# The last output of a state-space scan with a maxout layer: the products of the differences first, and four separate places for the result

## The chip, the cores and the metric

The kernel runs on one core of a Trainium2 chip. Its time is the device time of one execution in microseconds (us). The core has five engines with a queue of instructions each: TensorE (PE in the profile; its weight loads are listed apart, as PEld), VectorE (DVE), ScalarE (ACT), GpSimd (POOL) and SyncE (SP, which here issues the transfers). Matmuls write to PSUM, an accumulator memory of eight banks of 128 partitions by 2 KB; the other data are in SBUF. Transfers to and from the main memory go over 16 DMA engines. The profile is of one execution, and its times are counted from the start of the span, that is from the first recorded instruction.

## The reference

Two layers follow each other. The first is a scan over 768 tokens of 4 sequences with 8 heads, done in chunks; the second is a feed-forward layer that takes the maximum of three projections:

```python
# first layer, for each chunk, in outline
y[:, :, sl] = y_intra + y_inter              # (batch 4, heads 8, seq 768, head_dim 32)
state = decay_full * state + sum_j(B_j x_j decay_from_j)

# bridge: 4 x 768 tokens of 8 * 32 = 256 numbers
x = y.transpose(0, 2, 1, 3).reshape(3072, 256)

# second layer: w1, w2, w3 are 256 x 768, w_out is 768 x 256
h = np.maximum(np.maximum(x @ w1, x @ w2), x @ w3)
out = h @ w_out                              # 3072 x 256, float32
```

The change touches only the last product, `h @ w_out`, and only for the last 128 tokens of each of the four sequences.

## The kernel before

The kernel takes the 768 tokens in six chunks of 128 (`NC = 6`, `c = 0` to 5). A chunk holds 128 tokens of all four sequences (`NB = 4`), 512 in all. For each chunk it scans, makes the three projections in 36 units, takes the maximum (tiles `m`, 128 by 512, with four buffers), and makes six tiles of hidden values (`NF = 6`, 128 hidden values by 512 tokens each). Then come the products with `w_out`. The order of the work on every engine is the order of the program; it is written out by hand in short words (`FIRST`, `SECOND`, `STEADY`, `LAST`), and semaphores hold an instruction back until its data and its place are there.

From chunk 1 on, products are made from split operands. A hidden tile (`hidden`, L642) becomes three: a high part `hi` = value times a number just below one (ScalarE, L645), a low part `lo` = value less `hi` (VectorE, L648), and a difference `d` = `hi` less `lo` divided by TAU (VectorE, L639). The weights have the same three parts. In the code they are numbered 0 (`hi`), 1 (`lo`) and 2 (`d`). The result is (products of parts 0 and 1, less KAPPA times the products of part 2), times BACK; KAPPA and BACK are constants.

For chunks 1 to 4, "Y" steps make the products of part 2, ScalarE scales the bank in place, and "X" steps add the products of parts 0 and 1; `put` scales and stores. The last chunk's output is made by `last_down` (L787). It has one PSUM bank for each sequence, as two halves of 128 tokens by 256 outputs: `o[:, 0]` collects the products of parts 0 and 1, `o[:, 1]` those of part 2. It goes twice over the four sequences: first with hidden tiles 0 to 3 (12 matmuls for each sequence), then with tiles 4 and 5 (6 for each). In the second round each sequence is finished in turn:

- ScalarE reads `o[:, 0]`, scales it and writes it to `ob` in SBUF (L802),
- VectorE reads `o[:, 1]`, scales it, adds `ob`, and writes `ob` (L803),
- SP issues a store of 128 by 256 numbers, 128 KB (L806).

The tag "ob" has two buffers, so sequences 0 and 1 write to two places, and sequences 2 and 3 to the same two again. The tag "m" has four buffers, one taken by each hidden tile in turn; the last four takers before `last_down` are hidden tiles 2, 3, 4 and 5. Nothing follows `last_down` in the program.

Of the kernel before, what the change touches and what calls it, by code (L numbers as in the profile page):

```python
# [9 lines left out]
FP32 = mybir.dt.float32  # L10
# [3 lines left out]
AF = mybir.ActivationFunctionType  # L14
ALU = mybir.AluOpType
# [5 lines left out]
def kernel(  # L21
# [20 lines left out]
    nc = tc.nc  # L42

    NB, NH, S, D = x.shape
    N = B.shape[-1]
    P = 128
# [7 lines left out]
    DM, DF = moe_w1.shape  # L54
    KD = DM // P
    NF = DF // P
    BLK = NB * P
# [14 lines left out]
    KAPPA = TAU / (1.0 + TAU)  # L72
    HIGH = 1.0 - 2.0 ** -13
    BACK = ((1.0 + TAU) / TAU) ** 2
# [9 lines left out]
    ffn = ctx.enter_context(tc.tile_pool(name="ffn", bufs=2))  # L84
# [17 lines left out]
    def att_bank(shape, name):  # L102
        turn["att"] += 1
        if shared["att"] and turn["att"] % 5 == 0:
            return bank("sumA", 1, shape, name)
        return bank("att", 4, shape, name)

    def ffn_bank(shape, name):
        turn["ffn"] += 1
        if shared["ffn"] and turn["ffn"] % 3:  # L110
            return bank("sumB", 2, shape, name)
        return bank("ffn", 1, shape, name)
# [4 lines left out]
    for k in range(REP):  # L117
# [5 lines left out]
        out=a_sb,  # L123
        in_=a_rows.rearrange("r (c i) -> (r c) i", i=P).rearrange("(w r) i -> r w i", w=2))
# [4 lines left out]
            name=nc.get_next_instruction_name(),  # L129
# [23 lines left out]
    NW = 3 * NQ  # L153
# [22 lines left out]
    hs, h0 = {}, {}  # L176
# [103 lines left out]
    def weight_part(k, j, row, cols):  # L280
        return parts[k][j][:, row, cols]
# [14 lines left out]
        out=pick, in_=ident.rearrange("p (r k) -> p k r", k=BH), op=ALU.add, axis=AX.X)  # L296
    npick = const.tile([P, BH], FP32, name="npick")
    nc.vector.tensor_scalar(
        out=npick, in0=pick, scalar1=-1.0, scalar2=None, op0=ALU.mult)
# [4 lines left out]
        out=hsel, in_=hsel, pattern=[[-N, NH]], compare_op=ALU.is_ge, fill=0.0,  # L304
        base=0, channel_multiplier=1)
    nc.gpsimd.affine_select(
        out=hsel, in_=hsel, pattern=[[N, NH]], compare_op=ALU.is_ge, fill=0.0,
# [3 lines left out]
        out=parity, in_=hsel.rearrange("p (r g) -> p g r", g=2), op=ALU.add, axis=AX.X)  # L311
# [6 lines left out]
        out=mask, in_=mask, pattern=[[1, P]], compare_op=ALU.is_ge, fill=MASKED,  # L318
# [377 lines left out]
    opened, m, ready = {}, {}, set()  # L696
# [51 lines left out]
    def tokens(b):  # L748
        return slice(b * P, (b + 1) * P)
# [37 lines left out]
    def last_down():  # L787

        c = NC - 1
        os_ = [att_bank([P, 2, DM], "o") for _ in range(NB)]  # L790
        for fs in (range(NF - 2), range(NF - 2, NF)):
            for b, o in enumerate(os_):
                for f in fs:
                    for p in (2, 0, 1):
                        nc.tensor.matmul(  # L795
                            out=o[:, p // 2], lhsT=hs[f][p][:, tokens(b)],
                            rhs=weight_part(NW + f // 2, p, f % 2, slice(0, DM)),
                            start=(f == 0 and p == 2), stop=(f == NF - 1 and p > 0),
                            skip_group_check=True)
                if fs[-1] == NF - 1:  # L800
                    ob = ffn.tile([P, 2, DM], FP32, tag="ob", name="ob")[:, 0]
                    nc.scalar.activation(ob, o[:, 0], AF.Copy, scale=BACK)  # L802
                    nc.vector.scalar_tensor_tensor(  # L803
                        out=ob, in0=o[:, 1], scalar=-KAPPA * BACK, in1=ob, op0=ALU.mult,
                        op1=ALU.add)
                    nc.sync.dma_start(  # L806
                        out=out.rearrange("(b s) m -> s b m", s=S)[c * P:(c + 1) * P, b], in_=ob)

    for b in range(2, NB):
        below(b)  # L810
# [20 lines left out]
        out=cums.rearrange("k c s -> (k c) s").rearrange("(w r) s -> r w s", w=2), in_=a_sb)  # L831
# [219 lines left out]
    for n in range(NF * 3):  # L1051
        j, g = divmod(n, 2)
        q, i = divmod(j, 3)
        f = 2 * q + g
# [7 lines left out]
        if j > 0:  # L1062
            p = ffn_bank([P, BLK], "up")
            whole_group(p, i, f)
        else:
            p = pair[g]
# [3 lines left out]
        else:  # L1070
            if i == 2:
                h0[f] = hidden_place(NF - 2 + f // 3, f % 3, FP32)
            nc.vector.tensor_tensor(
                out=m[g] if i == 1 else h0[f], in0=m[g], in1=p, op=ALU.max)
# [22 lines left out]
    for steps in (tops, tails):  # L1097
        while steps:
            take(steps)
    last_down()  # L1100


# [28 lines left out]
```

## Time and profile before

| what | us |
|---|---|
| median of 4 runs (lowest, highest) | 279.46 (278.15, 282.49) |
| the profiled execution's own time | 279.69 |
| its span, first to last instruction | 277.9 |
| TensorE busy | 262.6 (94%) |
| ScalarE busy | 187.8 (68%) |
| VectorE busy | 180.7 (65%) |
| GpSimd busy | 72.1 (26%) |
| ScalarE's step of the last output, each of four (L802) | 0.383 |
| VectorE's step of the last output, each of four (L803) | 0.424 |
| last four stores, from issue to landing | 1.7 |

The busy times overlap, since the engines work side by side; a share of the span says little by itself. What sets the end is the chain of waits: it is followed back from the last instruction, at each step to what released it. A row of the chain or of the timeline gives the start in us from the start of the span, the length in us, the engine, the line of the kernel and the tile. "PE o L795" is a matmul into the banks of the last output, "ACT ob L802" and "DVE ob L803" are the two steps after it. In a view of waits, a row gives who waited, on whom, the sum in us, how often, and the longest. In a table of windows, a row has the stretch, its length, the busy time and the number of instructions of PE, PEld, DVE, ACT and POOL, the granted clock of TensorE, the mean share of the DMA engines that was busy, and the GB/s that they moved.

### The profile page before, as it was taken

The numbers are of one execution on the slowest core, as the hardware profiler recorded it, in microseconds if no ns is written. First come the engines' busy times: TensorE is split into PE (matmuls) and PEld (weight loads), VectorE is DVE, ScalarE is ACT, GpSimd is POOL, SyncE is SP. The second block draws the span as 40 slices with busy tenths as digits, with TensorE's granted clock in tenths as the row PEclk, the third lists the DMA queues.
The fourth block names the chain that finished last, engine by engine and source line by source line (L and its number), as shares of the span: only waits on it lengthen the run. The fifth ranks groups of instructions, "written<-read, shape, count | busy, mean of one in ns | idle before, by whom it ended". The sixth has DMA issues, their size and how long they took to land.

```text
span 277.9 us, 5404 instructions
## 1 busy us (share of the span) xinstructions
PE 262.6 (94%) x2054; PEld 205.4 (74%) x2054; DVE 180.7 (65%) x292; ACT 187.8 (68%) x423; POOL 72.1 (26%) x72
## 2 busy tenths in 40 slices
PE   6886799999999999999999999999999999999992
PEld 4663344438887787889888889888789788898892
DVE  2584577999476699573478852578760876713942
ACT  2774759891999999936699745799653854425612
POOL 5173915555973362216000333000000000000000
PEclk9999599999999999999999999999999999999999
DMA  7989989979992285688340793200001100002002
GB/s 83 179 290 287 283 138 167 224 171 224 173 230 55 62 97 72 91 203 125 95 62 0 146 239 32 78 0 2 1 0 40 39 2 0 0 2 75 2 0 75
DMA packets 105049, 28.13 MB, mean 101 GB/s; under 512 B 75328, under 2 KB 101952, under 8 KB 105024
## 3 DMA queue, kind: packets, MB, share of 16 engines
q1 hardware_dynamic: 104720, 27.66, 48.9%
q8 instruction: 16, 0.26, 0.4%
q10 hardware_dynamic: 304, 0.13, 0.2%
q14 instruction: 9, 0.07, 0.1%
HBM read 24.54 MB, written 3.24 MB: 100 GB/s over the span
## 4 chain that ended last, share of the span: by engine, by line
PE 85%; DMA 6%; ACT 3%; DVE 3%; issue 1%; ACTq 0%; SPq 0%; DVEq 0%
PE up L728 30%; PE up L706 15%; PE o L770 12%; PE up L665 7%; PE o L765 4%; PE y L598 3%; DMA rb<-in_moe_w_dram 3%; PE s L566 3%; PE o L795 3%; PE y L589 2%; DMA cums<-a_sb 2%; PE spread L396 1%; PE trB L493 1%; PE trC L493 1%; PE A L534 1%
## 5 line engine op out<-in xcount | busy, mean ns | idle before, releaser
L728 PE MATMUL up<-six,wp 128*128 128x512 f32 x360 | 95.8, 393 | 0.0
L728 PEld LDWEIGHTS up<-six,wp 128*128 128x128 f32 x360 | 66.6, 188 | 14.7 <-ACT six L625 0.6
L742 DVE TENSOR_TENSOR m<-m,up 128x512 f32<-128x512 f32 x60 | 40.4, 684 | 46.7 <-PE up L728 46.1
L692 ACT ACTIVATE up<-up 128x512 f32<-128x512 f32 x90 | 50.9, 582 | 19.5 <-PE up L706 19.3
L706 PE MATMUL up<-six,wd 128*128 128x512 f32 x180 | 53.9, 399 | 0.0
L467 ACT ACTIVATE L<-L,ncums 128x128 f32<-128x128 f32 x160 | 50.3, 394 | 0.0
L706 PEld LDWEIGHTS up<-six,wd 128*128 128x128 f32 x180 | 32.7, 188 | 8.7 <-DVE m L742 1.9
L574 DVE TENSOR_TENSOR L<-s,L 128x512 f32<-128x512 f32 x46 | 30.0, 682 | 2.1 <-issue 1.3
L665 PE MATMUL up<-six,w 128*128 128x512 f32 x64 | 30.8, 632 | 0.0
L460 POOL TENSOR_SCALAR_AFFINE_SELECT L<-L 128x1024 f32<-128x1024 f32 x20 | 21.9, 1120 | 12.4 <-DMA L<-cums 12.4
L770 PE MATMUL o<-wp,h 128*128 128x256 f32 x192 | 23.7, 283 | 0.0
L770 PEld LDWEIGHTS o<-wp,h 128*128 128x128 f32 x192 | 23.4, 192 | 0.1
L665 PEld LDWEIGHTS up<-six,w 128*128 128x128 f32 x64 | 12.7, 205 | 14.5 <-issue 13.5
L225 POOL TENSOR_TENSOR h<-h,h 128x512 uint32<-128x512 uint32 x12 | 16.1, 1345 | 23.8 <-DVE h L219 18.5
L639 DVE SCALAR_TENSOR_TENSOR h<-h,h 128x512 fp32r<-128x512 f32 x30 | 20.8, 692 | 1.0
L648 DVE TENSOR_TENSOR h<-m,h 128x512 fp32r<-128x512 f32 x30 | 20.8, 694 | 0.0
L645 ACT ACTIVATE h<-m 128x512 fp32r<-128x512 f32 x30 | 18.5, 629 | 3.0 <-DVE m L742 3.0
L783 ACT ACTIVATE ob<-o 128x512 f32<-128x512 f32 x10 | 6.0, 597 | 19.9 <-PE o L770 16.2
L566 PE MATMUL s<-six,six 32*128 32x256 f32 x192 | 15.2, 401 | 1.4 <-ACT six L508 1.4
L740 DVE COPY m<-up 128x512 f32<-128x512 f32 x14 | 9.6, 689 | 9.2 <-PE up L728 9.1
L566 PEld LDWEIGHTS s<-six,six 32*128 32x128 f32 x192 | 9.8, 184 | 6.7 <-issue 3.6
L770 PEld LDWEIGHTS o<-wd,h 128*128 128x128 f32 x96 | 12.6, 190 | 0.6
(101 smaller groups left out, 319.7 us busy)
## 6 DMA issues: line engine op xcount, KB each, us to landing
L<-cums SPq DMA_DIRECT2D x10, 1024.0 KB, 10.5
rb<-in_moe_w_dram SPq DMA_DIRECT2D x9, 512.0 KB, 6.4
raw_x<-in_x_dram SPq DMA_DIRECT2D x6, 512.0 KB, 10.4
out_dram<-ob SPq DMA_DIRECT2D x10, 256.0 KB, 2.1
raw_B<-in_B_dram SPq DMA_DIRECT2D x6, 256.0 KB, 4.5
raw_C<-in_C_dram SPq DMA_DIRECT2D x6, 256.0 KB, 6.3
rb<-in_moe_w_out_dram SPq DMA_DIRECT2D x3, 512.0 KB, 4.8
E<-cums SPq DMA_DIRECT2D x40, 32.0 KB, 2.4
```

What stands on the lines that cost most here:

```text
L460: nc.gpsimd.affine_select(out=Ls[c][:, b], in_=Ls[c][:, b], pattern=[[0, NH], [1, P]], compare_op=ALU.is_ge, fill=MASKED, base=0, channel_ ...
L467: nc.scalar.activation(L[:, b, h], L[:, b, h], AF.Exp, bias=ncum[c][:, b * NH + h:b * NH + h + 1], scale=1.0)
L566: nc.tensor.matmul(out=s[:, i].rearrange("j g i -> j (g i)"), lhsT=st["BT"][rows, b], rhs=st["CT"][rows, :, b], start=(i == 0), stop=True, ...
L574: nc.vector.tensor_tensor(out=M, in0=s, in1=M, op=ALU.mult)
L639: nc.vector.scalar_tensor_tensor(out=out, in0=lo.bitcast(FP32), scalar=-1.0 / TAU, in1=hi.bitcast(FP32), op0=ALU.mult, op1=ALU.add)
L648: nc.vector.tensor_tensor(out=lo, in0=src, in1=hi.bitcast(FP32), op=ALU.subtract)
L665: nc.tensor.matmul(out=bank, lhsT=whole[3 * (f // 2) + i][:, k, f % 2 * P:(f % 2 + 1) * P], rhs=yT[0][:, k], start=(k == 0), stop=(k == KD ...
L692: nc.scalar.activation(bank, bank, AF.Copy, scale=-KAPPA)
L706: nc.tensor.matmul(out=o, lhsT=weight_part(k, 2, kk, cols), rhs=yT[c][2][:, kk], start=(kk == 0), stop=(kk == KD - 1), skip_group_check=True)
L728: nc.tensor.matmul(out=o, lhsT=weight_part(k, j, kk, cols), rhs=yT[c][j][:, kk], start=False, stop=(kk == KD - 1 and j == 1), skip_group_c ...
L742: nc.vector.tensor_tensor(out=m[g], in0=m[g], in1=o, op=ALU.max)
L770: nc.tensor.matmul(out=o[:, b % 2], lhsT=hs[f][p][:, tokens(b)], rhs=weight_part(NW + f // 2, p, f % 2, slice(0, DM)), start=(first and p ...
```

## The change

The second round is cut into two passes over the four sequences. The first pass makes, for each sequence, the two products of part 2 for tiles 4 and 5, and ScalarE scales `o[:, 1]` into a place of its own in SBUF. The second pass makes the four products of parts 0 and 1 for each sequence; VectorE scales `o[:, 0]`, adds what ScalarE left, and the store is issued. The places are the first 256 columns of four tiles of the tag "m", so each sequence has its own. The round over tiles 0 to 3 is the same. The same 72 matmuls, four ScalarE steps, four VectorE steps and four stores are issued.

```diff
         os_ = [att_bank([P, 2, DM], "o") for _ in range(NB)]
-        for fs in (range(NF - 2), range(NF - 2, NF)):
-            for b, o in enumerate(os_):
-                for f in fs:
-                    for p in (2, 0, 1):
-                        nc.tensor.matmul(
-                            out=o[:, p // 2], lhsT=hs[f][p][:, tokens(b)],
...
-                if fs[-1] == NF - 1:
-                    ob = ffn.tile([P, 2, DM], FP32, tag="ob", name="ob")[:, 0]
-                    nc.scalar.activation(ob, o[:, 0], AF.Copy, scale=BACK)
-                    nc.vector.scalar_tensor_tensor(
-                        out=ob, in0=o[:, 1], scalar=-KAPPA * BACK, in1=ob, op0=ALU.mult,
-                        op1=ALU.add)
-                    nc.sync.dma_start(
-                        out=out.rearrange("(b s) m -> s b m", s=S)[c * P:(c + 1) * P, b], in_=ob)
+        obs = {}
+
+        def products(b, fs, ps_):
+            o = os_[b]
+            for f in fs:
+                for p in ps_:
+                    nc.tensor.matmul(
+                        out=o[:, p // 2], lhsT=hs[f][p][:, tokens(b)],
...
+        for b in range(NB):
+            products(b, range(NF - 2), (2, 0, 1))
+        for b, o in enumerate(os_):
+            products(b, range(NF - 2, NF), (2,))
+            obs[b] = ffn.tile([P, BLK], FP32, tag="m", bufs=4, name="m")[:, 0:DM]
+            nc.scalar.activation(obs[b], o[:, 1], AF.Copy, scale=-KAPPA * BACK)
+        for b, o in enumerate(os_):
+            products(b, range(NF - 2, NF), (0, 1))
+            nc.vector.scalar_tensor_tensor(
+                out=obs[b], in0=o[:, 0], scalar=BACK, in1=obs[b], op0=ALU.mult, op1=ALU.add)
+            nc.sync.dma_start(
+                out=out.rearrange("(b s) m -> s b m", s=S)[c * P:(c + 1) * P, b], in_=obs[b])
```

More of the change, by code (lines that the diff above doesn't have):

```diff
@@ L790, in last_down @@
         os_ = [att_bank([P, 2, DM], "o") for _ in range(NB)]
-        for fs in (range(NF - 2), range(NF - 2, NF)):
-            for b, o in enumerate(os_):
-                for f in fs:
-                    for p in (2, 0, 1):
-                        nc.tensor.matmul(
-                            out=o[:, p // 2], lhsT=hs[f][p][:, tokens(b)],
-                            rhs=weight_part(NW + f // 2, p, f % 2, slice(0, DM)),
-                            start=(f == 0 and p == 2), stop=(f == NF - 1 and p > 0),
-                            skip_group_check=True)
-                if fs[-1] == NF - 1:
-                    ob = ffn.tile([P, 2, DM], FP32, tag="ob", name="ob")[:, 0]
-                    nc.scalar.activation(ob, o[:, 0], AF.Copy, scale=BACK)
-                    nc.vector.scalar_tensor_tensor(
-                        out=ob, in0=o[:, 1], scalar=-KAPPA * BACK, in1=ob, op0=ALU.mult,
-                        op1=ALU.add)
-                    nc.sync.dma_start(
-                        out=out.rearrange("(b s) m -> s b m", s=S)[c * P:(c + 1) * P, b], in_=ob)
+        obs = {}
[5 more added lines that the diff above has]
+                        out=o[:, p // 2], lhsT=hs[f][p][:, tokens(b)],
+                        rhs=weight_part(NW + f // 2, p, f % 2, slice(0, DM)),
+                        start=(f == 0 and p == 2), stop=(f == NF - 1 and p > 0),
+                        skip_group_check=True)
+        for b in range(NB):
[10 more added lines that the diff above has]
+                out=out.rearrange("(b s) m -> s b m", s=S)[c * P:(c + 1) * P, b], in_=obs[b])
     for b in range(2, NB):
```

## The prediction, made before the changed kernel was run

> **What bounds the kernel now.** I read the page first, then the chain of waits from 264 us to the end, then the rows of the last microseconds and the shares of the DMA engines there. The change touches only the function that makes the last output, so the body of the kernel matters only in what it hands over to it.
>
> ```profile
> span 277.9 us, 5404 instructions
> ...
> PE 85%; DMA 6%; ACT 3%; DVE 3%; issue 1%; ACTq 0%; SPq 0%; DVEq 0%
> ```
>
> TensorE carries 85% of the chain that ends last. The change neither adds nor drops a matmul, so a gain can only come out of what follows the last one. The chain there, with start, length and what:
>
> ```profile
> 264.36 7.21 PE o L795 x60
> 271.57 0.02 issue
> 271.59 0.39 ACT ob L802
> 271.99 0.02 issue
> 272.01 0.43 DVE ob L803
> 272.44 0.02 issue
> 272.46 1.72 DMA out_dram<-ob
> 274.18 0.02 issue
> 274.20 0.04 ACTq L802
> 274.23 0.05 issue
> 274.28 0.39 ACT ob L802
> 274.67 0.02 issue
> 274.69 0.42 DVE ob L803
> ```
>
> Read it backwards. The last VectorE step starts at 274.69, because its ScalarE step started at 274.28, because the store of sequence 1 landed at 274.18: sequence 3 writes into the place that this store was reading. The chain leaves TensorE at sequence 1, though TensorE still worked for 2 and 3. The view of waits has the same twice, once for each of the two last sequences:
>
> ```profile
> ACT ob L802 <- PE o L795: 5.5, 2, 5.1
> ...
> ACT ob L802 <- DMA out_dram<-ob: 1.9, 2, 1.6
> ```
>
> The rows show where TensorE's second round over the four sequences begins and ends, and when the last difference that it needs is made:
>
> ```profile
> 267.05 0.69 DVE L639 SCALAR_TENSOR_TENSOR h<-h,h 128x512 fp32r<-128x512 f32 x1
> ```
>
> ```profile
> 269.95 0.28 PE L795 MATMUL o<-wd,h 128*128 128x256 f32 x1
> ...
> 272.59 0.40 PE L795 MATMUL o<-wp,h 128*128 128x256 f32 x2
> ```
>
> The second round is 24 matmuls, 0.12 us apart from 269.95; the last starts at 272.71 and ends at 272.59 + 0.40 = 272.99. The last four stores, against the ten before them (the number at the end is us from issue to landing), and the DMA engines' share while the very last two move (the two last columns):
>
> ```profile
> out_dram<-ob SPq DMA_DIRECT2D x10, 256.0 KB, 2.1
> ...
> out_dram<-ob SPq DMA_DIRECT2D x4, 128.0 KB, 1.7
> ```
>
> ```profile
> 275.20:275.80 0.60, 0.00 (x0) 0.00 (x0) 0.00 (x0) 0.00 (x0) 0.00 (x0) 1.00 0.64 219
> 275.80:276.50 0.70, 0.00 (x0) 0.00 (x0) 0.00 (x0) 0.00 (x0) 0.00 (x0) 1.00 0.55 187
> ```
>
> One store keeps all 16 engines busy for 0.60 x 0.64 = 0.38 us, or 0.70 x 0.55 = 0.39 us.
>
> **The change part by part.** *Removed: the wait for a place.* Today 274.28 - 272.99 = 1.29 us lie between TensorE's end and the last ScalarE step; with four places it goes. What the new places wait for instead: the ring "m" has four buffers, and the next four are those of hidden tiles 2, 3, 4 and 5. The last reader of tile 5 is the first of the two VectorE steps that make its low part and its difference; the second starts at 267.05, so the place is free by then, more than three microseconds before its first new writer. Nothing is late here.
>
> *Moved: the ScalarE step.* Four steps of 0.383 us (row of L802), of the same shape and still from PSUM, now scale the second half of each bank as soon as its two products are in. The pair of sequence 0 starts at 269.95 and 270.07, so ends at 270.07 + 0.28 = 270.35. ScalarE follows TensorE by 0.04 today (last product of sequence 0 at 270.55, end 270.83, ScalarE at 270.87), so it works from 270.39 to 270.77. The others follow at most 0.40 apart and end by 271.17, 271.57 and 271.97. No other work is queued on ScalarE. In the tail, 0.38 + 0.03 us go (274.28 to 274.69).
>
> *Added: TensorE waits for ScalarE.* The products into the first half of a bank now come after ScalarE's read of its second half, and the built program holds them back by a semaphore per sequence. Queued behind that wait are all remaining products, so each stall moves the end. The four groups would start at 270.91, 271.39, 271.87 and 272.35 (eight matmuls of 0.12 after 269.95, then four each), and their weights are loaded 0.11 earlier (268.04 before 268.15), so the waits are asked at 270.80, 271.28, 271.76 and 272.24. ScalarE is done at 270.77, 271.17, 271.57 and 271.97. Only the first is close. A release from ScalarE to a weight load took 0.05 us (ScalarE at 70.10 for 0.58, load at 70.73), so the load starts at 270.82: 0.02 us late. Bounds: nothing, if the loads stand further ahead; 0.20 us, the longest idle of TensorE's loads behind ScalarE in this trace (at 226.35). I take 0.02, by the release row, which is the same handover.
>
> The rule that speaks against this part is in the Trainium skill, "PSUM — Partial Sum Buffer", section "PSUM bank collisions raise a hardware error": two engines are to be kept apart by bank, not by address, so the half that nobody reads is locked as well. By the rule the sum has that 0.02 us, by a guard of bytes it would have none; no run here shows a collision.
>
> *Moved: the products of the differences.* The difference of hidden tile 5 is needed by the second matmul of the round instead of the fourth, 0.24 us earlier, at 270.07. It is ready at 267.05 + 0.69 = 267.74, so 2.3 us cover it; without them, TensorE would wait 0.24 us. Running several products into one half of a bank costs nothing: the 12 products of each "Y" step (L770) take 1.43 us on the chain, 0.12 each.
>
> *Changed: VectorE's step.* Same count, form (PSUM and SBUF in, SBUF out) and 0.424 us. It now waits directly for its sequence's last product, and these end 0.48 apart, longer than 0.424, so VectorE keeps up; nothing else is behind these steps. VectorE follows TensorE by 0.04 (TensorE leaves L728 at 264.36, L742 starts at 264.40).
>
> *Stores.* Four, 128 KB each, still the last on SP's queue in the same order, behind nothing new; POOL's queue is empty. Issues come 0.48 apart; one takes SP 0.33 to 0.35 us. Each keeps the engines busy 0.39 us, so each is through before the next, and the last should land 1.72 us after its issue, as now. Bounds: 1.7, the shortest store row, and 3.2, the longest of all fourteen stores. I take 1.72, since the 256 KB stores, with twice the bytes, have a median of 2.1.
>
> The page "DMA: Bandwidth & Descriptors" of the Trainium skill, section "Latency and other measured facts", speaks against it: access to HBM takes 0.2 us on average and 2 us at high load. If four stores in a row were high load, by that page the landing would grow by 1.8 us and the sum would turn to about 0.2 us slower; the trace's four stores have 1.7 us in pairs 0.7 apart, and nothing shows four.
>
> **Sum.** Last product 272.99 + 0.02 = 273.01; VectorE from 273.05 to 273.47; issue, 0.04 later as now (274.69 + 0.42, then 275.15), at 273.51; before it was 275.15. Saved: 1.64 us. Landing and the closing stretch keep their length, so the span is 277.9 - 1.64 = 276.3 and the profiled execution's 279.69 becomes 278.05. That execution lies 0.23 above the median of the four runs (279.46), which gives 277.82. I write 277.9, -0.56%. A measurement of this kernel can tell about 0.5% from no change, here 1.40 us, so even a complete success clears that bound by only 0.24 us.
>
> **The rivals.** *B: part is given back.* If the stall is 0.20 at the first wait, or the last landing rises from 1.72 to the 2.1 of the larger stores, the saving is 1.64 - 0.18 = 1.46 or 1.64 - 0.38 = 1.26; both together give 1.08, so 278.4. For it: the first wait is short by hundredths, four stores follow each other. Against it: the DMA engines have 0.09 us of slack per store. With a landing of 3.2 the saving is 0.16, and the time 279.3.
>
> *C: the change does not free the tail.* If the new places were held by late readers, the wait would only change its name. Were ScalarE's step of sequence 3 held as now, to 274.28, the time would stay 279.4. Against it: the readers of the ring end about 267.05, and no store reads it.
>
> *D: the last store lands much later and it ends slower.* One mechanism: four stores of 128 KB in flight in 1.5 us make the last wait for the earlier ones. It breaks even at a landing of 1.72 + 1.64 = 3.36 us and is slower by 0.5% from 4.76. The only row so long is E<-cums, eight loads issued in 3.70 us with landings of 2.0 / 2.4 / 8.1 us; 8.1 would mean 284.2. Against it: the median there is 2.4, even with a denser queue.
>
> **How the numbers follow.** Full effect (A) 0.74, B 0.15, C 0.06, D 0.05. Within A the gain is so near the bound that the spread of the runs (three of them within 278.15 to 279.69) puts about a sixth of it, 0.12, below 0.5%. So faster 0.62, same 0.12 + 0.15 + 0.06 = 0.33, slower 0.05. Low end: the fastest run shown, 278.15, less the gain without any stall, 1.66, is 276.5; I take 276.6. High end: the worst landing of B, 279.3; I take 279.2, which leaves out C, D and little more.
>
> **What would show it.** ScalarE's four steps start about 270.39 and wait for products alone; no wait on the stores is left. VectorE's steps stand 0.48 apart, the last at 273.05. Stores are issued 0.48 apart. The chain runs from TensorE to VectorE to the last store. Wrong would be: idle time on TensorE between 270.8 and 272.4, a last landing above 2 us, or a closing stretch that isn't the 1.05 us between landing (275.15 + 1.72 = 276.87) and the end.

## The result and the profile after

The changed kernel has a median of 278.32 us (43 runs, 276.57 to 280.96), the kernel before one of 280.01 us in the runs made beside it (64 runs, 277.89 to 282.49). The ratio is 0.9945, with a 95% interval of 0.9923 to 0.9966: faster by 0.55%, where 0.56% was forecast. The ratio leaves out executions more than 1.5% above the fastest of their kernel, so it isn't quite that of the two medians (0.9940).

The profiled execution of the changed kernel took 280.31 us, with a span of 278.6, and so is longer than the 279.69 and 277.9 of before. It can't be compared as a whole: the clock that TensorE was granted differs between executions, and in this one it was low early on. The rows of the granted clock (40 equal slices of the span, tenths of full speed), first of the changed kernel and then of before, show where:

```profile
PEclk9965989999999999999999999999999999999999
```

```profile
PEclk9999599999999999999999999999999999999999
```

TensorE reached its second round over the four sequences at 272.16, 2.2 us later than before (269.95). All of that lag comes from the early stretch, where the clock rows differ: the first matmul of L706 starts at 71.5 us against 69.3, the last of L770 at 254.9 against 252.7. From 45 us to the end of TensorE's work the clock is full in both. So the traces are compared from there: T is the start of the second round, in each kernel's own trace. Before, the span ended at T+7.96; now it ends at T+6.44. The gain is 1.52 us, 0.54% of 280.01, well within the interval of the times (0.34% to 0.77%). Forecast was 1.64.

The chain of waits of the changed kernel from 264 us on (start, length, what):

```profile
266.56 6.01 PE o L797 x50
272.57 0.02 issue
272.60 0.26 ACT m L808
...
273.88 0.42 DVE m L811
274.30 0.01 DVEq L811
274.31 0.04 issue
274.35 0.42 DVE m L811
...
275.31 0.42 DVE m L811
```

No transfer stands in it any more. It ends in four VectorE steps, 0.48 us apart. The same stretch as rows of the timeline:

```profile
272.16 1.12 PE L797 MATMUL o<-wd,h 128*128 128x256 f32 x8
272.60 1.24 ACT L808 ACTIVATE m<-o 128x256 f32<-128x256 f32 x4 [4.64 <-PE o L797]
273.11 2.09 PE L797 MATMUL o<-wp,h 128*128 128x256 f32 x16
273.88 1.85 DVE L811 SCALAR_TENSOR_TENSOR m<-o,m 128x256 f32<-128x256 f32 x4 [3.93 <-ACT m L808]
274.33 1.81 SPq L813 DMA_DIRECT2D out_dram<-m  x4
```

TensorE runs from 272.16 to 275.20 (273.11 + 2.09), 3.04 us, as long as before: the wait for ScalarE costs it at most 0.02. ScalarE's four steps run side by side with it. The brackets name ScalarE as what VectorE waited for, but ScalarE was done at 273.84 (272.60 + 1.24) at the latest and the four VectorE steps end 0.48 apart, which is TensorE's pace of four products. They wait for two engines, and one more row tells of that: a wait instruction of its own stands before each of the four.

```profile
L811 DVEq EVENT_SEMAPHORE  x4: 21/21/21, 273.8 to 275.2; - x4
```

The last product ended at 275.20 and the last VectorE step started at 275.31: 0.11 us, where I had counted on 0.04. The stores (the number at the end is us from issue to landing) took a little longer than the 1.7 of before:

```profile
out_dram<-m SPq DMA_DIRECT2D x4, 128.0 KB, 1.8
```

### The profile page after: what moved, and what is told of

Read it like the earlier page. It is cut to its first block, busy times and chain, and to the rows that moved or that the text cites. A ratio compares the mean times of both kernels' runs of the same rounds, so it can differ in the third digit from the quotient of the medians.

```text
span 278.6 us, 5401 instructions
## 1 busy us (share of the span) xinstructions
PE 266.2 (96%) x2054; PEld 207.4 (74%) x2054; DVE 182.3 (65%) x292; ACT 187.3 (67%) x423; POOL 72.7 (26%) x72
## 4 chain that ended last, share of the span: by engine, by line
PE 89%; ACT 4%; DVE 4%; issue 1%; POOL 0%; ACTq 0%; POOLq 0%; DVEq 0%
PE up L728 30%; PE up L706 15%; PE o L770 12%; PE up L665 7%; PE s L566 4%; PE o L765 4%; PE y L598 3%; PE o L797 2%; PE y L589 2%; PE up L657 2%; PE spread L396 1%; PE y L609 1%; DVE L L574 1%; PE A L534 1%; PE trB L493 1%
## 5 line engine op out<-in xcount | busy, mean ns | idle before, releaser
L706 PE MATMUL up<-six,wd 128*128 128x512 f32 x180 | 54.0, 399 | 0.0
L706 PEld LDWEIGHTS up<-six,wd 128*128 128x128 f32 x180 | 32.7, 188 | 8.7 <-DVE m L742 1.9
L460 POOL TENSOR_SCALAR_AFFINE_SELECT L<-L 128x1024 f32<-128x1024 f32 x20 | 22.8, 1167 | 9.1 <-DMA L<-cums 9.1
L770 PE MATMUL o<-wp,h 128*128 128x256 f32 x192 | 23.7, 283 | 0.0
L770 PEld LDWEIGHTS o<-wp,h 128*128 128x128 f32 x192 | 23.4, 192 | 0.1
L566 PE MATMUL s<-six,six 32*128 32x256 f32 x192 | 16.2, 412 | 1.4 <-ACT six L508 1.4
L770 PEld LDWEIGHTS o<-wd,h 128*128 128x128 f32 x96 | 12.6, 190 | 0.6
```

Of the source, the lines that this page charges most:

```text
L460: nc.gpsimd.affine_select(out=Ls[c][:, b], in_=Ls[c][:, b], pattern=[[0, NH], [1, P]], compare_op=ALU.is_ge, fill=MASKED, base=0, channel_ ...
L566: nc.tensor.matmul(out=s[:, i].rearrange("j g i -> j (g i)"), lhsT=st["BT"][rows, b], rhs=st["CT"][rows, :, b], start=(i == 0), stop=True, ...
L706: nc.tensor.matmul(out=o, lhsT=weight_part(k, 2, kk, cols), rhs=yT[c][2][:, kk], start=(kk == 0), stop=(kk == KD - 1), skip_group_check=True)
L770: nc.tensor.matmul(out=o[:, b % 2], lhsT=hs[f][p][:, tokens(b)], rhs=weight_part(NW + f // 2, p, f % 2, slice(0, DM)), start=(first and p ...
```

## The experiments

All are read from T, in us; "expected" is the end that stood in the expectation of the theory, and for the changed kernel 7.96 less the 1.64 of the prediction.

| kernel | last product ends | last VectorE step starts | last store issued | landed | end | expected |
|---|---|---|---|---|---|---|
| before | 3.04 | 4.74 | 5.19 | 6.88 | 7.96 | |
| changed | 3.04 | 3.15 | 3.60 | 5.37 | 6.44 | 6.32 |
| places alone | 3.04 | 3.49 | 3.95 | 5.63 | 6.70 | 6.77 |
| order alone | 5.64 | 5.74 | 6.19 | 7.89 | 8.96 | 9.1 |
| one sequence at a time | 6.02 | 6.13 | 6.58 | 8.28 | 9.35 | 9.4 |
| ScalarE's step twice | 4.10 | 4.21 | 4.66 | 6.35 | 7.42 | 7.0 |
| one store | 3.05 | 3.15 | 3.61 | 5.32 | 6.20 | 6.4 |
| early look | 3.05 | 3.08 | 3.63 | 5.41 | 6.49 | 6.37 or 6.44 |
| places in "ob" | 3.05 | 3.15 | 3.60 | 5.36 | 6.43 | 6.44 |
| last wait | 3.05 | 3.15 | 3.61 | 5.37 | 6.20 | 6.19 |
| all three | 3.04 | 3.08 | 3.54 | 5.28 | 6.12 | 6.12 |

**Four places alone.**

```diff
-                    ob = ffn.tile([P, 2, DM], FP32, tag="ob", name="ob")[:, 0]
+                    ob = ffn.tile([P, BLK], FP32, tag="m", bufs=4, name="m")[:, 0:DM]
```

> Four places alone, the old order kept: sequences in turn, ScalarE then VectorE after each sequence's last product. Measured from the first matmul of the second round (T): before, the last VectorE step starts at T+4.74 and the span ends at T+7.95; in the changed kernel T+3.15 and T+6.44. Theory (the tail is last product, VectorE, store, closing stretch): the wait for a landing goes, ScalarE's step stays on the chain. Last product ends T+3.04, ScalarE T+3.08 to 3.46, VectorE T+3.49 to 3.91, issue T+3.95, end T+6.77; 1.2 us faster than before, 278.6 on 279.8, ratio 0.996. Rival 'the order carries the gain': little or nothing is gained, end T+7.5 or later. Rival 'the places carry it all': end T+6.44.

The end came at T+6.70, 1.26 us earlier than before; in time the ratio was 0.9937 (0.9897 to 0.9977). The places carry most of the gain, and the chain then runs as expected: last product, ScalarE's step, VectorE's step, store.

**The order alone.** Two places as before; since the places of sequences 2 and 3 come free only with stores 0 and 1, their ScalarE steps have to stand behind these.

```diff
+        def scale(b):
+            obs[b] = ffn.tile([P, 2, DM], FP32, tag="ob", name="ob")[:, 0]
+            nc.scalar.activation(obs[b], os_[b][:, 1], AF.Copy, scale=-KAPPA * BACK)
...
             products(b, range(NF - 2, NF), (2,))
-            obs[b] = ffn.tile([P, BLK], FP32, tag="m", bufs=4, name="m")[:, 0:DM]
-            nc.scalar.activation(obs[b], o[:, 1], AF.Copy, scale=-KAPPA * BACK)
+            if b < 2:
+                scale(b)
...
                 out=out.rearrange("(b s) m -> s b m", s=S)[c * P:(c + 1) * P, b], in_=obs[b])
+            if b < 2:
+                scale(b + 2)
```

> The new order alone, with two places as before; the ScalarE steps of sequences 2 and 3 stand behind the stores of 0 and 1. Theory: ScalarE of sequence 2 waits for the landing of store 0 and TensorE's last products for that ScalarE step. Store 0 issued at about T+2.2, landed T+3.9; ScalarE T+4.0 to 4.4; products of sequence 2 start T+4.6, of sequence 3 at T+5.05, end T+5.7; last VectorE step starts T+5.8, span ends T+9.1: 1.1 us slower than before, ratio 1.004, and some 2.6 us slower than with four places. Rival 'the order carries the gain': faster than before, end below T+7.5.

```profile
276.35 0.85 ACT L807 ACTIVATE ob<-o 128x256 f32<-128x256 f32 x2 [2.89 <-DMA out_dram<-ob]
276.78 1.22 PE L797 MATMUL o<-wp,h 128*128 128x256 f32 x8 [2.33 <-ACT ob L807]
```

Now the wait for a landing stands in front of TensorE's last eight products instead of behind them: TensorE idles 2.33 us, and the end is 1.00 us later than before. In time that isn't told from no change (ratio 1.0012, 0.997 to 1.0054), so the direction rests on the trace. The two parts are not two gains that add up: the order alone loses 1.00 us, and with four places it brings 0.26 (6.70 to 6.44).

**One sequence at a time.** Four places and, within each sequence, the products of the differences first, but no other sequence in between.

```diff
             nc.scalar.activation(obs[b], o[:, 1], AF.Copy, scale=-KAPPA * BACK)
-        for b, o in enumerate(os_):
             products(b, range(NF - 2, NF), (0, 1))
```

> Four places, and the products of the differences first within each sequence, but the four sequences in turn: two products of part 2, ScalarE's step, four products of parts 0 and 1, VectorE, store, then the next sequence. Theory (TensorE is held by bank until ScalarE has read the other half, and nothing else is queued to cover it): per sequence the first two products end 0.40 after their start, ScalarE runs 0.44 to 0.82, weights load at 0.87, the four products start at 0.98 and the next sequence at 1.46, where 0.72 is the pace without a wait. Last VectorE step at T+6.1, end T+9.4: 1.45 us slower than before, ratio 1.005. Rival (no hold by bank, or the queue of weight loads hides it): last step T+3.15, end T+6.44.

```profile
272.75 0.74 PE L797 MATMUL o<-wp,h 128*128 128x256 f32 x4 [0.47 <-ACT m L808]
274.26 0.74 PE L797 MATMUL o<-wp,h 128*128 128x256 f32 x4 [0.53 <-ACT m L808]
...
277.16 0.74 PE L797 MATMUL o<-wp,h 128*128 128x256 f32 x4 [0.47 <-ACT m L808]
```

TensorE idles about 0.5 us before each group of products, and a sequence takes 1.45 to 1.51 us instead of 0.72. The last product ends 2.98 us later; the end is 1.39 us later than before (time: ratio 1.0068, 1.0017 to 1.0119). This is the price of the wait for ScalarE with nothing to cover it, 0.75 us for each sequence. What hides it in the changed kernel is that the first pass goes over all four sequences: six other products of part 2 lie between.

**ScalarE's step twice**, to find how much of that cover there is.

```diff
             nc.scalar.activation(obs[b], o[:, 1], AF.Copy, scale=-KAPPA * BACK)
+            nc.scalar.activation(obs[b], o[:, 1], AF.Copy, scale=-KAPPA * BACK)
```

> The changed kernel with each of the four ScalarE steps done twice, into the same place with the same values. Theory (the added wait of TensorE for ScalarE is covered by a margin of some hundredths at the first sequence and 0.2 to 0.6 at the others): ScalarE paces at 0.286 a step in the changed kernel, so the pairs are done at T+1.11, 1.68, 2.25 and 2.82; the loads were due at T+0.87, 1.35, 1.83 and 2.31; TensorE stalls 0.29, then 0.09 three times. Last VectorE step at T+3.7, end T+7.0. Rival (the wait is not on TensorE's path at all): T+3.15 and T+6.44.

```profile
269.92 2.81 PE L797 MATMUL o<-wp,h 128*128 128x256 f32 x16 [0.17 <-ACT m L809]
```

The sixteen products took 2.81 us instead of 2.09: TensorE now follows ScalarE. For sequence 0 nothing of the cover is left over: ScalarE ended 0.42 us later than in the changed kernel (T+1.24 against T+0.82), and so did the four products (T+2.03 against T+1.62). Each of the three other sequences added 0.21, the 0.69 of a pair of steps less the 0.48 of four products. The stall was sized too low (1.06 us in place of 0.56), because the second step of a pair writes where the first wrote and starts only after it has ended: its start lies 0.41 us after the first's, and I had counted 0.286. A pair takes 0.69, and 0.69 is the pace of VectorE's steps here (T+2.14, 2.84, 3.52, 4.21).

**Places elsewhere.** Two "ob" buffers, both halves used, instead of four of the ring "m".

```diff
-            obs[b] = ffn.tile([P, BLK], FP32, tag="m", bufs=4, name="m")[:, 0:DM]
+            if b % 2 == 0:
+                ob = ffn.tile([P, 2, DM], FP32, tag="ob", name="ob")
+            obs[b] = ob[:, b % 2]
```

> The changed kernel with its four places as the two halves of two 'ob' buffers, none from the ring 'm'. Theory (the ring's older readers are long done, any four places serve): last VectorE step at T+3.15, end T+6.44, the same time as the changed kernel, ratio to before 0.9945. Rival 'the places in the ring hold something back': 0.05 us or more earlier.

T+6.43; in time 0.9907 (0.9865 to 0.9949), an interval that holds the changed kernel's ratio. Any four places serve, and the ring's older readers hold nothing back.

**One store.**

```diff
-            nc.sync.dma_start(
-                out=out.rearrange("(b s) m -> s b m", s=S)[c * P:(c + 1) * P, b], in_=obs[b])
+            if b == NB - 1:
+                nc.sync.dma_start(
+                    out=out.rearrange("(b s) m -> s b m", s=S)[c * P:(c + 1) * P, b], in_=obs[b])
```

> The changed kernel with the store of sequence 3 alone; the outputs of the last 128 tokens of sequences 0 to 2 are left out. Theory (four stores 0.48 us apart do not hold each other up): the lone store lands 1.7 us after its issue and the end stays at T+6.4, at most 0.05 earlier. Rival D of the prediction (stores in flight make the last one late): the landing is 0.1 us or more shorter than the 1.8 of the changed kernel's stores, the end at T+6.3 or earlier.

The two signs disagreed. The end came at T+6.20, 0.24 us earlier, as the rival had it. But the lone store took 1.72 us and the fourth of four 1.76, so only 0.04 lies in the transfer, as the theory had it. The other 0.2 lie behind the landing: the closing stretch was 0.88 us (5.32 to 6.20) instead of 1.07. The rows of SP's wait instructions at the end, first of the changed kernel and then of this one (shortest, median and longest in ns, then first and last start):

```profile
L1133 SPq EVENT_SEMAPHORE  x7: 17/27/28, 277.5 to 278.5; - x7
```

```profile
L1134 SPq EVENT_SEMAPHORE  x7: 17/27/1165, 276.0 to 278.2; - x7
```

In the changed kernel all seven follow the landing (277.5). Here three are over before it, and one of 1165 ns spans it. That gave a new theory, which the next run tells from the rival.

**The last wait.** Loads of the last chunk cut in pieces move the last store four places on in the turn of the eight semaphores.

```diff
+        n = {"B": 2, "C": 4}.get(name, 1) if c == NC - 1 else 1
+        for k in range(n):
+            bs = slice(k * NB // n, (k + 1) * NB // n)
-        nc.sync.dma_start(
-            out=t, in_=src[:, :, c * P:(c + 1) * P, :].rearrange("b h s n -> s (b h) n"))
+            nc.sync.dma_start(
+                out=t[:, bs.start * NH:bs.stop * NH],
+                in_=src[bs, :, c * P:(c + 1) * P, :].rearrange("b h s n -> s (b h) n"))
```

> The changed kernel with two of the last chunk's loads cut in pieces (B in two, C in four), which only moves the last store four places on among the eight semaphores that the stores and loads take in turn. At the end SP waits for all of them with five wait instructions, 0.06 us each; in the changed kernel the first of the five is the one for the last store, and the other four follow after the landing; in this kernel it stands in the fifth. Theory (the four waits after the landing are part of the closing stretch): last VectorE step T+3.15, landing T+5.37, as in the changed kernel, but the end at T+6.19 instead of T+6.44. It also explains why the kernel with one store, whose semaphore stood in the fourth wait, ended 0.24 earlier with a landing only 0.05 shorter. Rival (the lone store ended early because no other stores were in flight): T+6.44 here.

```profile
L1137 SPq EVENT_SEMAPHORE  x7: 17/28/28, 274.4 to 276.5; - x7
```

All four stores are there, the landing is at T+5.37 as in the changed kernel, and the end at T+6.20. T is 270.32 in this trace, so the landing is at 275.69, and SP's waits begin at 274.4, ahead of it. The 0.24 us are four wait instructions that stood behind the landing; other stores in flight cost some 0.04.

**An early look.** One column of sequence 3's place is copied by VectorE ahead of its four steps.

```diff
-            obs[b] = ffn.tile([P, BLK], FP32, tag="m", bufs=4, name="m")[:, 0:DM]
+            t = ffn.tile([P, BLK], FP32, tag="m", bufs=4, name="m")
+            obs[b], obs["spare"] = t[:, 0:DM], obs.get("spare", t[:, DM:DM + 1])
             nc.scalar.activation(obs[b], o[:, 1], AF.Copy, scale=-KAPPA * BACK)
+        nc.vector.tensor_copy(out=obs["spare"], in_=obs[NB - 1][:, 0:1])
         for b, o in enumerate(os_):
             products(b, range(NF - 2, NF), (0, 1))
```

> The changed kernel with one more VectorE instruction, a copy of one column of sequence 3's place, made before the four VectorE steps: it waits for ScalarE, so that the steps of sequences 0 to 2 wait for TensorE alone; the step of sequence 3 waits for that copy and TensorE. In the changed kernel each VectorE step waits for two engines and starts 0.11 to 0.13 us after its last product, where single waits took 0.04 us. Theory (the second wait costs it, since a wait instruction of its own stands before the step and is the one held for TensorE): steps of sequences 0 to 2 start 0.04 us after their last products; the last one starts T+3.08 if the wait for TensorE is the one on the step itself, T+3.15 if any second wait costs the same. End T+6.37 or T+6.44; in time 0.07 us, not measurable. Rival 'VectorE's start after a matmul into this bank simply takes 0.11': no step changes.

```profile
272.46 0.15 DVE L810 COPY m<-m 128x1 f32<-128x1 f32 x1 [3.92 <-ACT m L809]
272.53 1.73 DVE L813 SCALAR_TENSOR_TENSOR m<-o,m 128x256 f32<-128x256 f32 x4
```

The steps of sequences 1 to 3 start 0.04 us after their last products (the last at T+3.08), so the 0.07 is the second wait; only the step of sequence 0 starts later, since it stands behind the copy. Sequence 3 still has two waits, and pays nothing: what counts is which of them is the one on the step itself. But the end did not come earlier (T+6.49). The store whose data were ready at T+3.51 was issued at T+3.63, since SP was still busy with the one before (0.40 us each and 0.09 around it). The next thing in line was SP's queue. The six times (276.50 to 280.93) are too few to tell this kernel from the changed one.

**All three together**: the early look, the last wait, and the stores of sequences 1 and 3 from ScalarE's queue. The first two are the edits shown above; the third is this:

```diff
-            nc.sync.dma_start(
+            (nc.scalar if b % 2 else nc.sync).dma_start(
```

> The changed kernel with the early look of VectorE (one wait for each of its last steps), the stores of sequences 1 and 3 issued from ScalarE's queue, and the last store in the fifth of SP's final waits. In the kernel with the early look alone, the last VectorE step ended 0.07 earlier but the store was issued no earlier, since SP took 0.40 us for each issue and 0.09 around it. Theory (SP's queue was the next in line): last VectorE step T+3.08 to 3.51, issue T+3.54, landing T+5.29, end T+6.12, 1.84 us faster than before, ratio 0.9934. Rival (the stores land no earlier since the DMA engines take them one after another): landing at T+5.37 or later, end T+6.2.

Issue at T+3.54, landing at T+5.28, end at T+6.12: 1.84 us before the kernel before and 0.32 before the changed one. The times say little: three of six runs had a mean granted clock of 0.988 or more and took 275.63 to 277.70 us, the three others 0.975 or 0.976 and took 279.85 to 280.46. The ratio of 0.9865 (0.98 to 0.993) counts the first three alone; the median of all six, 278.78, is 0.9948 of that of before (280.23, 11 runs). The 0.32 us rest on the traces; the times can't tell this kernel from the changed one.

## Why the prediction was right, point by point

- *Removed: the wait for a place.* Right. No store is waited for, and the ring's readers were long done ("places in ob": 6.43 against 6.44).
- *Moved: ScalarE's step.* Right; it starts at T+0.44, as forecast (270.39 less 269.95). Its steps follow each other 0.26 to 0.30 us apart, not the 0.40 that I took as the upper bound, so the cover for TensorE's later waits is larger than counted.
- *Added: TensorE waits for ScalarE.* Right, in size too: 0.02 us or less, where 0.02 was forecast. The upper bound of 0.20 was none: it wasn't the longest idle time of the loads behind ScalarE in the trace of before (one is 5.5 us, at 29.79), and "one sequence at a time" has TensorE wait 0.47 to 0.53. The rule of the Trainium skill that I set against it ("PSUM — Partial Sum Buffer", "PSUM bank collisions raise a hardware error": keep two engines apart by bank) is what the program's waits do, and "one sequence at a time" shows what they cost without cover: 0.75 us for each sequence.
- *Moved: the products of the differences.* Right; the first eight products run 0.12 apart without a stop.
- *Changed: VectorE's step.* The mis-sized term. "VectorE follows TensorE by 0.04" came from a step that waits for no other engine than TensorE. This one waits for two, and follows by 0.11: 0.07 us lost. The trace of before had shown such a step: its matmul ends at 260.74 (260.12 + 0.62), and it starts 0.11 later, again with a wait instruction of its own in front.

```profile
260.12 0.62 PE L728 MATMUL up<-six,wp 128*128 128x512 f32 x2
260.84 0.69 DVE L742 TENSOR_TENSOR m<-m,up 128x512 f32<-128x512 f32 x1 [0.35 <-PE up L728]
```

- *Stores.* The last landing took 1.76 us; forecast 1.72, and 1.69 for the last store of before. The 1.72 was the store of sequence 1; with 1.69 the closing stretch of before is 1.07 us, not 1.05, and it kept its length. Against the 1.69, 0.07 us are lost, some 0.04 of them to the other stores in flight. The other page ("DMA: Bandwidth & Descriptors", "Latency and other measured facts": 2 us of access under high load) gave a slower kernel if four stores were high load; the trace does not agree: the four took 1.75 to 1.77 us, not 1.8 us more than before.
- *Sum.* 1.64 - 0.07 - 0.07 leaves 1.50, and 1.52 was measured: the 0.02 of the wait for ScalarE did not reach the last product (3.04 in both). The 0.12 us that are missing are less than either amount of rival B (0.18 and 0.38); its longer landing came, in small, its stall did not. Rival C is refuted by the changed kernel's chain, which has no transfer in it, and by "places in ob"; rival D by the 0.04 of "one store" and "last wait". The landing of 8.1 us that D rests on belongs to a load issued at 52.17, one of 40 in that row; the eight issued in 3.70 us landed in 2.2.
- *The time.* 277.9 was forecast, 278.32 measured. That the gain agrees to 0.01% is luck: the interval is 0.2% to either side, and the saving of 1.64 us was 0.12 too large, which rounding 277.82 up to 277.9 made up for in part. The level was off, since the median of before that I started from (279.46, four runs) was 280.01 in 64 runs. The doubt about 0.5% was justified: the interval, 0.34% to 0.77%, holds it, so the times don't say on which side of it the gain lies.

## What to carry to other kernels

When a store at the end is waited for because its buffer is reused, count the whole chain from the last product to the last store once for the present order and once for the new one. Test the two parts of such a change apart: here the places alone brought 1.26 of the 1.52 us, and the order alone lost 1.00, since it moved the wait for a place in front of the busiest engine. Before a wait is put on the busiest engine, look for the work that lies between the release and the request; here six products of other sequences covered a wait that costs 0.75 us each time when bare. When the last few tenths matter, look past the last landing: the order of the final waits was worth 0.24 us, about as much as the new order of the products once the places were there (0.26).

## What was not expected of the hardware

The time goes with how long TensorE is granted a low clock early in the run, and it falls into a few levels. In the eleven traces TensorE has half its clock for 13.6, 6.8 or 3.4 us while it still has products to make, all of it between 15 and 40 us, and the mean granted clock is 0.971 to 0.975, 0.986 to 0.988 or 0.992. The median span by the mean granted clock of each execution, of before (53 runs beside the experiments) and of the changed kernel:

| mean granted clock | before | changed | difference |
|---|---|---|---|
| below 0.980 | 280.0 (25 runs) | 278.6 (17) | 1.4 |
| 0.982 to 0.989 | 277.7 (22) | 276.2 (19) | 1.5 |
| 0.990 and above | 276.3 (6) | 275.15 (8) | 1.15 |

The levels lie 1 to 2.4 us apart, where the change is worth 1.5, and the gain appears in each. For a change at one place, the two traces, counted from a matmul just ahead of it, gave hundredths of a microsecond (T+6.44 and T+6.43 in two kernels with the same order); the times needed dozens of runs for a few tenths.

Two waits on one VectorE step cost 0.07 us more than one when the later release is the one held by the separate wait instruction, and nothing when it is the one on the step itself. SP took 0.33 to 0.35 us to issue a store of 128 KB alone or 0.66 us and more after the one before, and 0.35 to 0.40 when the next followed within 0.5 us.
